# Hedgehog attention and an S4 convolution in one launch: the kernel written anew with shared stages, one hand-placed SBUF buffer and two half-width passes

## The chip, the cores and the metric

The kernel runs on one core of one Trainium2 chip. The metric is the device time of one execution in microseconds; six runs of the kernel before have a median of 710.55 us (710.0 to 714.23).

## The reference

Two independent parts write the two halves of one output of 2048 rows by 896 columns (bf16).

Part A (columns 0 to 447) is linear attention with 16 heads of 28: `q, k, v = x @ wqkv`; per head `pq = q @ w_phi[h]`, `pk = k @ w_phi[h]`; the features are `[softmax(pq), softmax(-pq)]` and the same of pk; `kv = sum_s phi_k^T v`, `z = sum_s phi_k`; `o = (phi_q @ kv) / (phi_q @ z + 1e-6)`; the output is `o @ wo`.

Part B (columns 448 to 895) is a state-space convolution: for 448 channels and 256 states `K[d, l] = Re sum_n C[d,n] * dt*B[d,n] * exp(dt*A[d,n]*l)`, then `y = irfft(rfft(u) * rfft(K))` over the sequence with zero padding, plus `u * Dskip`. The positions l are rounded to bf16, so only 641 distinct values of l occur.

## The kernel before

`hedgehog_attention` (L86 to L425) runs first. Four transposing loads bring x in as xT (L165). Eight groups of projections make qT and kT with channels on partitions (L181), sixteen make v (L196). Keys: for each of 16 row tiles one product with the block-diagonal w_phi (L217), two exponentials (L226), a sum per head (L228), a reciprocal and a product (L233). Queries: products (L254), two exponentials over 2048 columns (L263), normalisers by a matmul with head indicators (L270), a reciprocal on 16 partitions (L279), a broadcast back by matmul (L288) and a product (L295). The state kv is formed in 512 small matmuls (L312), goes through DRAM to become block-diagonal (L321, L338 to L342), and the denominators take another 16-partition reciprocal (L366). Numerators (L382), scaling (L399) and the output projection (L409) end part A.

`ssm_conv` (L507 to L836) follows, with its own loads of parameters and of u (L537 to L551). It makes parameters (L562 to L586), powers of exp(dt*A) (L611 to L633), and the spectrum SU of u by matmuls with a table G (L655, L657). K's 641 values come from factors: 32 coarse powers U (`hi_tables`, L699, on VectorE) times 49 fine powers W (`table_args`, L666: TensorE multiplies the exponents, ScalarE applies Exp into E and Sin twice into W). This runs for four quarters of the columns (L723). In each, E and W are filled, W is multiplied by E (L727, "damping"), and 448 small matmuls per quarter (L738) form K into Ts. After the last quarter 28 small DMAs on SP's queue scatter Ts into Kt (L749, L751), matmuls with tables `ft` give K's spectrum SK (L773, L775), and VectorE multiplies spectra (L786 to L833) between two inverse transforms (`inverse`, L799; matmuls L811; output L814 to L820).

Order on each engine is set by a planner: instructions carry their place in the program as priority, and among those that its own model holds ready, the earliest in the program is queued next. At run time each engine takes its queue in order. Buffers are tiles of pools; a tile that reuses another's bytes waits for it.

Of the kernel before, what the change touches and what calls it, by code (L numbers as in the profile page):

```python
# [11 lines left out]
I32 = mybir.dt.int32  # L13
ACT = mybir.ActivationFunctionType
ALU = mybir.AluOpType
AX = mybir.AxisListType

S_LEN = 2048
# [16 lines left out]
def round_f32(nc, out_ap, in_ap):
    nc.vector.tensor_scalar(out_ap, in_ap, MAGIC_ROUND, -MAGIC_ROUND, op0=ALU.add, op1=ALU.add)


def floor_div_const(nc, pool, out_ap, in_ap, shape, P, tag):
    t = pool.tile(shape, F32, name="fdt", tag=tag)
    nc.vector.tensor_scalar(t, in_ap, 1.0 / float(P), 0.5 / float(P) - 0.5, op0=ALU.mult, op1=ALU.add)
    round_f32(nc, out_ap, t)


def _head_row_segments(h):
    r0, r1 = D_HEAD * h, D_HEAD * h + D_HEAD
    segs = []
    for ci, plo, phi, g0, g1 in CHUNKS:  # L50
        a, b = max(r0, g0), min(r1, g1)
        if a < b:
            segs.append((ci, plo + (a - g0), plo + (b - g0), a - r0, b - r0))
    return segs


@with_exitstack
def kernel(
    ctx: ExitStack,
    tc: tile.TileContext,  # L60
    A_x: bass.AP,
    A_wqkv: bass.AP,
    A_w_phi: bass.AP,
    A_wo: bass.AP,
    B_u: bass.AP,
    B_A_re: bass.AP,
    B_A_im: bass.AP,
    B_B_re: bass.AP,
    B_B_im: bass.AP,
    B_C_re: bass.AP,  # L70
    B_C_im: bass.AP,
    B_log_dt: bass.AP,
    B_Dskip: bass.AP,
    out: bass.AP,
    do_a: bool = True,
    do_b: bool = True,
):
    nc = tc.nc
    out2 = out[0]
    if do_a:  # L80
        hedgehog_attention(tc, A_x, A_wqkv, A_w_phi, A_wo, out2)
    if do_b:
        ssm_conv(tc, B_u, B_A_re, B_A_im, B_B_re, B_B_im, B_C_re, B_C_im, B_log_dt, B_Dskip, out2)


def hedgehog_attention(tc, A_x, A_wqkv, A_w_phi, A_wo, out2):  # L86
    nc = tc.nc
    x2 = A_x[0]
    const_pool = tc.alloc_tile_pool(name="a_const", bufs=1)
    wt_pool = tc.alloc_tile_pool(name="a_w", bufs=1)  # L90
    va_pool = tc.alloc_tile_pool(name="a_va", bufs=1)
    work_pool = tc.alloc_tile_pool(name="a_work", bufs=2)
    small_pool = tc.alloc_tile_pool(name="a_small", bufs=2)
    dram_pool = tc.alloc_tile_pool(name="a_dram", bufs=1, space=bass.MemoryType.DRAM)

    dma_engs = [nc.sync, nc.scalar]
    dcount = [0]

    def dma(out_ap, in_ap, eng=None):
        if eng is None:  # L100
            eng = dma_engs[dcount[0] % len(dma_engs)]
            dcount[0] += 1
        return eng.dma_start(out=out_ap, in_=in_ap)

    Wt = []
    for j in range(4):
        t = wt_pool.tile([128, 3 * D_MODEL], BF16, name=f"Wqkv{j}")
        ci, plo, phi, g0, g1 = CHUNKS[j]
        dma(t[plo:phi, :], A_wqkv[g0:g1, :])
        Wt.append(t)  # L110
    Wo = []
    for j in range(4):
        t = wt_pool.tile([128, D_MODEL], BF16, name=f"Wo{j}")
        ci, plo, phi, g0, g1 = CHUNKS[j]
        dma(t[plo:phi, :], A_wo[g0:g1, :])
        Wo.append(t)
    WBD = []
    for j in range(4):
        t = wt_pool.tile([128, D_MODEL], BF16, name=f"WBD{j}")
        nc.gpsimd.memset(t[:, :], 0.0)  # L120
        WBD.append(t)
    for h in range(N_HEAD):
        for ci, plo, phi, s0, s1 in _head_row_segments(h):
            dma(WBD[ci][plo:phi, D_HEAD * h:D_HEAD * h + D_HEAD], A_w_phi[h, s0:s1, :])
    INDT16 = const_pool.tile([N_HEAD, D_MODEL], BF16, name="INDT16")
    it_f = small_pool.tile([N_HEAD, D_MODEL], I32, name="it_f", tag="it_f")
    nc.gpsimd.iota(it_f[:, :], pattern=[[1, D_MODEL]], base=0, channel_multiplier=0)
    ff = small_pool.tile([N_HEAD, D_MODEL], F32, name="ff", tag="ff")
    nc.vector.tensor_copy(ff[:, :], it_f[:, :])
    hd16 = small_pool.tile([N_HEAD, D_MODEL], F32, name="hd16", tag="hd16")  # L130
    floor_div_const(nc, small_pool, hd16[:, :], ff[:, :], [N_HEAD, D_MODEL], D_HEAD, "fd16")
# [36 lines left out]
    qT = []
    kT = []
    with tc.tile_pool(name="ps_qkv", bufs=1, space=bass.MemoryType.PSUM) as ps_pool:  # L170
        for which in range(2):
            for fc in range(4):
                ci, plo, phi, g0, g1 = CHUNKS[fc]
                frows = phi - plo
                fcol0 = which * D_MODEL + g0
                pool = qk_pool if which == 0 else k_pool
                dst = pool.tile([128, S_LEN], BF16, name=("qT" if which == 0 else "kT") + str(fc))
                ps = ps_pool.tile([128, S_LEN], F32, name="ps_qk", tag="big")
                for sc in range(4):
# [12 lines left out]
                (qT if which == 0 else kT).append(dst)
# [18 lines left out]
    for sgn in (+1, -1):  # L211
        PHIK[sgn] = phi_pool.tile([128, 16, D_MODEL], BF16, name=f"PHIK{'p' if sgn>0 else 'n'}")
# [654 lines left out]
```

## Time and profile before

| what | value |
|---|---|
| median of six runs | 710.55 us |
| the profiled execution's own time | 710.85 us |
| its span, first to last instruction | 709.1 us |
| mean granted TensorE clock (1 is 2.4 GHz, 0.5 is 1.2 GHz) | 0.727 |
| busy: TensorE, VectorE, ScalarE, GpSimd | 375.4, 401.1, 257.7, 9.6 us |
| DMA traffic | 17.19 MB, mean 24 GB/s |

The span is read by stages: a time window gives each engine's busy time in it, and the engine nearest to the window's length, or the chain of waits where none is near, is its bound. The profiled execution took 1.75 us more than its span, outside the first and last instruction.

### The profile page before, as it was taken

The numbers are of one execution on the slowest core, as the hardware profiler recorded it, in microseconds if no ns is written. First come the engines' busy times: TensorE is split into PE (matmuls) and PEld (weight loads), VectorE is DVE, ScalarE is ACT, GpSimd is POOL, SyncE is SP. The second block draws the span as 40 slices with busy tenths as digits, with TensorE's granted clock in tenths as the row PEclk, the third lists the DMA queues.
The fourth block names the chain that finished last, engine by engine and source line by source line (L and its number), as shares of the span: only waits on it lengthen the run. The fifth ranks groups of instructions, "written<-read, shape, count | busy, mean of one in ns | idle before, by whom it ended". The sixth has DMA issues, their size and how long they took to land.

```text
span 709.1 us, 8560 instructions
## 1 busy us (share of the span) xinstructions
PE 375.4 (53%) x3530; PEld 178.0 (25%) x3536; DVE 401.1 (57%) x576; ACT 257.7 (36%) x415; POOL 9.6 (1%) x31
## 2 busy tenths in 40 slices
PE   0599766453458464992537903624534326097434
PEld 0122211110015211231212502613424315043211
DVE  2043399205695137336462199886986983058981
ACT  0012134430000001221829993993884961053000
POOL 2000000010000000000000000000000000000000
PEclk9999955555556665996666955956857857589867
DMA  5300000000000000017200000000000020230101
GB/s 137 73 1 0 0 1 0 0 0 0 0 1 4 6 1 0 1 66 225 77 14 0 1 0 1 3 0 2 2 0 2 2 103 3 30 108 1 52 0 52
DMA packets 26622, 17.19 MB, mean 24 GB/s; under 512 B 15904, under 2 KB 25368, under 8 KB 26456
## 3 DMA queue, kind: packets, MB, share of 16 engines
q1 hardware_dynamic: 19098, 13.94, 7.2%
q10 hardware_dynamic: 7486, 2.72, 1.5%
q8 instruction: 27, 0.44, 0.3%
q14 instruction: 11, 0.09, 0.0%
HBM read 10.25 MB, written 3.72 MB: 20 GB/s over the span
## 4 chain that ended last, share of the span: by engine, by line
PE 34%; DVE 26%; ACT 18%; DMA 9%; issue 6%; SPq 5%; ACTq 1%; DVEq 0%
ACT W L679 11%; DVE W L727 7%; PE ps_k L738 6%; PE ps_qk L181 5%; PE num_ps L382 3%; PE ps_s L773 3%; PE ps_pq L254 3%; DMA xT<-in_A_x_dram 2%; DVE zk L228 2%; SPq L749 2%; SPq L551 2%; PE ps_u L655 2%; PE ps_o L811 2%; PE ps_a L673 2%; PE zps L270 2%
## 5 line engine op out<-in xcount | busy, mean ns | idle before, releaser
L738 PE MATMUL ps_k<-W,U 128*32 128x49 bf16 x1792 | 44.1, 268 | 46.8 <-DVE W L727 40.9
L673 PE MATMUL ps_a<-TH,PID 128*128 128x224 bf16 x128 | 20.3, 323 | 71.4 <-ACT W L679 70.2
L398 ACT CAST rbc_sb<-rbc_ps 128x512 bf16<-128x512 f32 (+1 forms) x16 | 9.2, 584 | 133.9 <-PE rbc_ps L391 133.5
L738 PEld LDWEIGHTS <-U 128*32 128x32 bf16 x1792 | 41.2, 138 | 50.1 <-issue 44.6
L181 PE MATMUL ps_qk<-xT,Wqkv 128*128 128x512 bf16 (+3 forms) x125 | 37.2, 405 | 29.2 <-DMA xT<-in_A_x_dram 26.0
L679 ACT ACTIVATE W<-ps_a,bias_hp 128x896 bf16<-128x896 f32 (+2 forms) x76 | 51.2, 822 | 0.4
L727 DVE TENSOR_TENSOR W<-W,E 128x10976 bf16<-128x10976 bf16 x8 | 46.6, 5871 | 8.1 <-ACT W L679 8.1
L673 PEld LDWEIGHTS <-PID 128*128 128x128 bf16 x256 | 29.4, 117 | 81.7 <-issue 76.5
L655 PE MATMUL ps_u<-ab,G 128*128 128x448 bf16 x128 | 33.4, 413 | 25.4 <-ACT SU L657 17.6
L679 ACT ACTIVATE E<-ps_a 128x896 bf16<-128x896 f32 (+2 forms) x76 | 46.0, 719 | 1.4 <-PE ps_a L673 1.3
L679 ACT ACTIVATE W<-ps_a 128x896 bf16<-128x896 f32 (+2 forms) x76 | 44.7, 819 | 0.0
L811 PE MATMUL ps_o<-SD,G 128*128 128x448 bf16 x128 | 27.8, 382 | 25.9 <-DVE SD L801 25.9
L710 DVE TENSOR_TENSOR t<-U,PW 128x896 bf16<-128x896 bf16 (+3 forms) x56 | 37.8, 675 | 2.0
L711 DVE TENSOR_TENSOR t<-U,PW 128x896 bf16<-128x896 bf16 (+3 forms) x56 | 37.5, 669 | 0.0
L773 PE MATMUL ps_s<-Kt,ft 128*128 128x448 bf16 x112 | 24.5, 381 | 18.1 <-DMA Kt<-Ts 18.0
L217 PE MATMUL ps_pk<-WBD,kT 128*128 128x448 bf16 x64 | 25.2, 508 | 15.7 <-ACT ek L226 13.6
L786 DVE TENSOR_TENSOR t<-SU,SK 128x3584 bf16<-128x3584 bf16 x6 | 12.0, 2020 | 37.7 <-ACT SK L775 37.6
L254 PE MATMUL ps_pq<-qT,WBD 128*128 128x512 bf16 (+3 forms) x39 | 18.7, 609 | 15.0 <-ACT EQ_n L263 11.3
L226 ACT ACTIVATE ek<-ps_pk 128x448 bf16<-128x448 f32 x32 | 16.8, 543 | 25.8 <-DVE PHIKp L233 22.6
L775 ACT CAST SK<-ps_s 128x448 bf16<-128x448 f32 x32 | 15.5, 545 | 27.4 <-PE ps_s L773 27.4
L655 PEld LDWEIGHTS <-G 128*128 128x128 bf16 x128 | 14.0, 110 | 42.6 <-issue 35.3
L181 PEld LDWEIGHTS <-Wqkv 128*128 128x128 bf16 (+3 forms) x128 | 11.0, 101 | 54.7 <-issue 46.1
(141 smaller groups left out, 627.2 us busy)
## 6 DMA issues: line engine op xcount, KB each, us to landing
ft<-dft_f SPq DMA_DIRECT2D x4, 896.0 KB
G<-dft_g SPq DMA_DIRECT2D x1, 1024.0 KB
out_dram<-osb ACTq DMA_DIRECT2D x8, 112.0 KB
out_dram<-osb SPq DMA_DIRECT2D x8, 112.0 KB
UD<-in_B_u_dram SPq DMA_DIRECT2D x4, 224.0 KB
UD<-in_B_u_dram SPq DMA_DIRECT2D x8, 112.0 KB
out_dram<-ob SPq DMA_DIRECT2D x4, 224.0 KB
out_dram<-ob SPq DMA_DIRECT2D x8, 112.0 KB
```

The costliest lines, as they stand in the source:

```text
L181: nc.tensor.matmul(ps[plo:phi, sc * 512:(sc + 1) * 512], lhsT=Wt[dci][dplo:dphi, fcol0:fcol0 + frows], rhs=xT[dci][dplo:dphi, sc * 512:(sc ...
L217: nc.tensor.matmul(ps[:, 0:D_MODEL], lhsT=kT[dci][dplo:dphi, tt * 128:(tt + 1) * 128], rhs=WBD[dci][dplo:dphi, 0:D_MODEL], start=(dj == 0) ...
L254: nc.tensor.matmul(ps[plo:phi, sc * 512:(sc + 1) * 512], lhsT=WBD[dci][dplo:dphi, g0:g0 + frows], rhs=qT[dci][dplo:dphi, sc * 512:(sc + 1) ...
L655: nc.tensor.matmul(ps[:, 0:D_MODEL], lhsT=G[:, cp, jt, 128 * mt:128 * mt + 128], rhs=ab[:, b, cp ^ st, jt, :], start=(jt == 0), stop=(jt = ...
L673: nc.tensor.matmul(o, lhsT=PID[:, 4 * grp + e, :], rhs=src[:, part, q0:q0 + 2 * COLS], start=(part == 0), stop=(part == 1))
L679: act(out_ap, in_ap, fn, scale=float(sgn * s), **kw)
L710: TT(out=t1[:, 0:n], in0=src, in1=bc(0), op=ALU.mult)
L711: TT(out=t2[:, 0:n], in0=src, in1=bc(1), op=ALU.mult)
L727: TT(out=W[:, ri, :, :], in0=W[:, ri, :, :], in1=E[:, :, :], op=ALU.mult)
L738: nc.tensor.matmul(ps[32 * g:32 * g + 32, qq * N_LO:(qq + 1) * N_LO], lhsT=U[:, :, ri, x], rhs=W[:, ri, :, (c % 2) * COLS + x], start=(i = ...
L773: nc.tensor.matmul(ps[:, 0:D_MODEL], lhsT=ft[:, fi, 128 * mt:128 * mt + 128], rhs=Kt[:, kt, :], start=(n == 0), stop=(n == len(terms) - 1))
L811: nc.tensor.matmul(ps[:, 0:D_MODEL], lhsT=G[:, cp, mt, 128 * jt:128 * jt + 128], rhs=S[:, r, cp, mt, :], start=(cp == 0 and mt == 0), stop ...
```

## The change

Nearly every line of the kernel's body is replaced; the two functions become one. What differs, in program order (names as in the new code):

1. **Buffers.** All of SBUF is one tile; `Bytes` cuts views of it at byte offsets chosen by hand, so that views of different stages lie on the same bytes. PSUM pools of a later stage wait per tile.
2. **Queues.** ACT's queue loads the state-space parameters, SP's the transposed x, GpSimd's the tables and weights; wo and G wait on GpSimd's queue for the last transpose.
3. **Weights folded.** `fold_weights` multiplies w_phi into the q and k columns of wqkv; q and k themselves are no longer formed.
4. **Keys.** One loop over 16 row tiles makes pk, v, both exponentials, one sum over both signs, and v divided by the sums; kv and z accumulate in one PSUM tile over the tiles, and a head mask makes them block-diagonal. No DRAM, no 512 small matmuls.
5. **SU** is stored to DRAM (`SUd`) in two halves of channels and read back late.
6. **Queries** keep plain exponentials; normalisers and denominators are formed with rows on partitions (128 matmuls of 8 columns), and one scale per row, sign and head (SC) goes into the numerators.
7. **Quarters.** `hi_tables` works once per quarter on 224 columns in place of twice on 112. Damping is cut into ten pieces issued as groups of W are finished. U has two buffers. The argument tiles still have two PSUM buffers.
8. **Halves.** After quarters 0-1 and 2-3 a half of the channels is scattered (24 + 4 DMAs, the 24 alternating between SP's and GpSimd's queue), and `kernel_spectrum` and `conv_half` work on 224 columns each; the first spectrum stands in the program behind the third quarter.
9. **Convolution.** u*Dskip is added by an identity matmul into PSUM and ScalarE evicts; u is read a second time on GpSimd's queue, 12 loads, into bytes of W.

The diff, cut to what the prediction speaks of:

```diff
+    sb = Bytes(sb_pool.tile([128, 211136 // 2], BF16, name="sbuf"))
+    ps_mm = ctx.enter_context(tc.tile_pool(name="ps_mm", bufs=2, space=bass.MemoryType.PSUM))
+    ps_a = tc.alloc_tile_pool(name="ps_a", bufs=1, space=bass.MemoryType.PSUM, reuse_waits="tile")
...
+    for k in (32, 64, 128):
+        for key, src in (("a", AT), ("t", TH)):
+            for half in range(2):
...
+                if key == "a":
+                    act(amp[:, hc], p[:, 0:D_MODEL], ACT.Exp, scale=float(k))
+                else:
+                    act(cs[:, 0, hc], p[:, 0:D_MODEL], ACT.Sin, scale=float(k), bias=bias_hp[:, :])
+                    act(cs[:, 1, hc], p[:, 0:D_MODEL], ACT.Sin, scale=float(-k))
...
+    acc = ps_a.tile([112, 2, 512], F32, name="acc", tag="acc")
+    for tt in range(16):
+        ts = slice(128 * tt, 128 * tt + 128)
+        pk = ps_a.tile([128, 512], F32, name="pk", tag="pk", bufs=2)
+        pv = ps_a.tile([128, 512], F32, name="pv", tag="pv", bufs=2)
+        for dj in range(4):
+            mm(pk[:, 0:D_MODEL], lhsT=xT[dj][:, ts], rhs=WpK[:, dj, :], start=(dj == 0), stop=(dj == 3))
+            mm(pv[:, 0:D_MODEL], lhsT=xT[dj][:, ts], rhs=wv[:, dj, :], start=(dj == 0), stop=(dj == 3))
+        EK = sb("EK", [128, 2, D_MODEL], BF16, oEK, bufs=2)
+        for s in range(2):
+            act(EK[:, s, :], pk[:, 0:D_MODEL], ACT.Exp, scale=1.0 - 2.0 * s)
+        zk = sb("zk", [128, 2, 16], F32, 10496, bufs=1)
+        nc.vector.tensor_reduce(zk[:, :, :], EK[:, :, :].rearrange("p s (h f) -> p s h f", f=D_HEAD), axis=AX.X,
+                                op=ALU.add)
+        nc.vector.reciprocal(rk[:, :, :], zk[:, :, :])
...
+        TT(out=VR[:, :, :, 0:D_HEAD],
+           in0=pv[:, 0:D_MODEL].rearrange("p (h d) -> p h d", d=D_HEAD).unsqueeze(1).to_broadcast(
+               [128, 2, 16, D_HEAD]),
+           in1=rk[:, :, :].unsqueeze(3).to_broadcast([128, 2, 16, D_HEAD]), op=ALU.mult)
...
+    for tt in range(16):
+        pn = ps_a.tile([128, 2, 512], F32, name="pn", tag="acc")
+        for s in range(2):
+            for c in range(4):
+                mm(pn[:, s, 112 * c:112 * c + 112], lhsT=EQ[:, s, c, ts], rhs=KVN[:, s, c, :, :],
+                   start=True, stop=True)
+        on = sb("on", [128, 2, D_MODEL], BF16, 0, bufs=2)
+        TT(out=on[:, :, :].rearrange("p s (h d) -> p s h d", d=D_HEAD),
+           in0=pn[:, :, 0:D_MODEL].rearrange("p s (h d) -> p s h d", d=D_HEAD),
+           in1=SC[:, tt].unsqueeze(3).to_broadcast([128, 2, 16, D_HEAD]), op=ALU.mult)
+        po = mmt([112, 4, 128])
+        for c in range(4):
+            for s in range(2):
+                mm(po[:, c, :], lhsT=on[:, s, 112 * c:112 * c + 112], rhs=ident, start=(s == 0), stop=(s == 1))
...
+    def damp_after(grp):
+        if grp == 0:
+            damp([slice(0, 4), slice(16, 20), slice(24, 32), slice(36, 40), slice(44, 49)])
+        elif grp == 1:
+            damp([slice(4, 8), slice(20, 24), slice(32, 36), slice(40, 44)])
+        elif grp == 3:
+            damp([slice(8, 16)])
...
+    for qt in range(4):
+        h = qt // 2
...
+        table_args(AT, qt, [E], [(ACT.Exp, None)], lambda g: None)
+        U = hi_tables(qt)
+        table_args(TH, qt, [W[:, 0], W[:, 1]], [(ACT.Sin, bias_hp[:, :]), (ACT.Sin, None)], damp_after)
+        build_k(qt, U, Ts)
+        if qt == 2:
+            kernel_spectrum(0, SKs[0])
+            nc.sync.dma_start(out=SUs[0][:, :, :, :, :, :], in_=SUd[:, 0])
...
+        if qt % 2 == 1:
+            scatter_k(h, Ts)
+            SK = sb(f"SK{h}", [128, 2, 2, 2, 4, HW], BF16, (oSK0, oW)[h])
+            if h == 1:
+                kernel_spectrum(h, SK)
...
+            UD = sb("UD", [128, 2, 2, 4, D_MODEL], BF16, oW + 14336)
...
+        for t in range(4):
+            nc.gpsimd.dma_start(out=UD[:, b, 1, t, :], in_=pair_rows(u2, 1024 * b, t, 0))
...
+    for h in range(2):
+        conv_half(h, SUs[h], SKs[h], UD, G2, OB)
```

## Rows read from the trace of the kernel before

**Rows 1.** The page: busy time by engine, and the chain's shares by engine.
```profile
PE 375.4 (53%) x3530; PEld 178.0 (25%) x3536; DVE 401.1 (57%) x576; ACT 257.7 (36%) x415; POOL 9.6 (1%) x31
...
PE 34%; DVE 26%; ACT 18%; DMA 9%; issue 6%; SPq 5%; ACTq 1%; DVEq 0%
```

**Rows 2.** Windows: length, busy us (count) PE, PEld, DVE, ACT, POOL; clock, DMA.
```profile
82.00:326.00 244.00, 148.85 (x870) 48.11 (x872) 122.23 (x183) 46.70 (x65) 3.36 (x8) 0.66 0.03 9
326.00:408.00 82.00, 45.34 (x232) 23.96 (x233) 37.78 (x68) 54.30 (x84) 1.21 (x4) 0.73 0.21 59
408.00:602.00 194.00, 75.97 (x2000) 65.39 (x1999) 157.23 (x229) 133.85 (x230) 0.00 (x0) 0.68 0.03 11
602.00:644.00 42.00, 23.95 (x118) 11.12 (x110) 12.13 (x8) 14.41 (x30) 0.00 (x0) 0.76 0.24 58
644.00:709.10 65.10, 28.50 (x132) 13.51 (x130) 48.66 (x45) 1.53 (x4) 0.00 (x0) 0.76 0.10 28
```

**Rows 3.** Timeline of one quarter: start, us, engine, line, operation, count, [idle before].
```profile
457.72 6.55 ACT L679 ACTIVATE W<-ps_a,bias_hp 128x896 bf16<-128x896 f32 x13
...
469.20 3.92 ACT L679 ACTIVATE W<-ps_a,bias_hp 128x896 bf16<-128x896 f32 x4
...
479.06 0.91 ACT L679 ACTIVATE W<-ps_a 128x896 bf16<-128x896 f32 x1
...
479.20 11.66 DVE L727 TENSOR_TENSOR W<-W,E 128x10976 bf16<-128x10976 bf16 x2 [2.69 <-ACT W L679]
...
490.91 3.70 PE L738 MATMUL ps_k<-W,U 128*32 128x49 bf16 x155 [5.40 <-DVE W L727]
...
503.30 1.71 PE L673 MATMUL ps_a<-AT,PID 128*128 128x224 bf16 x16
...
507.60 4.86 ACT L679 ACTIVATE W<-ps_a,bias_hp 128x896 bf16<-128x896 f32 x8
```

**Rows 4.** Groups by form: count | busy us, mean ns of one | idle before.
```profile
L711 DVE TENSOR_TENSOR t<-U,PW 128x1792 bf16<-128x1792 bf16 x16 | 17.4, 1085 | 0.0
...
L622 DVE TENSOR_TENSOR PW<-amp,cs 128x896 bf16<-128x896 f32 x4 | 4.1, 1086 | 0.0
...
L228 DVE TENSOR_REDUCE zk<-ek 128x16 f32<-128x448 bf16 x32 | 18.3, 614 | 9.7 <-ACT ek L226 9.7
...
L203 DVE CAST v_aug<-ps_v 128x448 bf16<-128x448 f32 x16 | 9.6, 622 | 14.8 <-PE ps_v L196 14.8
...
L232 DVE RECIPROCAL rzk<-zk 128x16 f32<-128x16 f32 x32 | 5.9, 226 | 0.0
...
L226 ACT ACTIVATE ek<-ps_pk 128x448 bf16<-128x448 f32 x32 | 16.8, 543 | 25.8 <-DVE PHIKp L233 22.6 <-PE ps_pk L217 3.1
...
L657 ACT CAST SU<-ps_u 128x448 bf16<-128x448 f32 x32 | 17.5, 588 | 4.7 <-PE ps_u L655 4.7
...
L679 ACT ACT_TABLE_LOAD x8 | 10.3, 1283 | 34.5 <-DVE W L727 33.7 <-PE ps_a L673 0.8
```

**Rows 5.** Timeline: TensorE runs whose length gives the pace of one matmul.
```profile
339.77 0.36 PE L584 MATMUL ps_t<-PID,natcr 112*128 112x112 bf16 x4
...
371.36 3.14 PE L655 MATMUL ps_u<-ab,G 128*128 128x448 bf16 x8 [12.36 <-ACT SU L657]
...
419.44 1.65 PE L673 MATMUL ps_a<-TH,PID 128*128 128x224 bf16 x8 [12.20 <-ACT W L679]
...
684.78 13.66 PE L811 MATMUL ps_o<-SD,G 128*128 128x448 bf16 x64 [21.56 <-DVE SD L801]
```

**Rows 6.** Timeline: what SP's queue needs to issue loads, scatter and outputs.
```profile
331.24 9.83 SPq L551 DMA_DIRECT2D UD<-in_B_u_dram  x4
...
602.66 4.14 SPq L749 DMA_DIRECT2D Kt<-Ts  x6
...
694.59 5.90 SPq L820 DMA_DIRECT2D out_dram<-ob  x4
```

**Rows 7.** Chain of waits, 0 to 30 us: start, us, what.
```profile
14.98 4.34 DMA xT<-in_A_x_dram
```

More of the change, by code (lines that the diff above doesn't have):

```diff
@@ L47, in _head_row_segments @@
[L47 to L83, printed above, removed]
@@ L504, in pair_rows, with __init__, __call__, kernel @@
                    ap=[[128 * rs, 2], [-2 * rs, 64], [1, D_MODEL]])
-def ssm_conv(tc, B_u, B_A_re, B_A_im, B_B_re, B_B_im, B_C_re, B_C_im, B_log_dt, B_Dskip, out2):
+class Bytes:
+    def __init__(self, tile_):
+        self.tile = tile_
+        self.turn = {}
+    def __call__(self, name, shape, dtype, off, bufs=1):
+        size = int(np.prod(shape[1:])) * (4 if dtype == F32 else 2)
+        turn = self.turn.get(name, 0)
+        self.turn[name] = turn + 1
+        a = (off + size * (turn % bufs)) // 2
+        v = self.tile[0:shape[0], a:a + size // 2]
+        if dtype == F32:
+            v = v.bitcast(F32)
+        names = "abcdefg"[:len(shape) - 1]
+        if len(names) > 1:
+            v = v.rearrange(f"p ({' '.join(names)}) -> p {' '.join(names)}",
+                            **{n: s for n, s in zip(names[1:], shape[2:])})
+        return v
+@with_exitstack
+def kernel(
+    ctx: ExitStack,
+    tc: tile.TileContext,
+    A_x: bass.AP,
+    A_wqkv: bass.AP,
+    A_w_phi: bass.AP,
+    A_wo: bass.AP,
+    B_u: bass.AP,
+    B_A_re: bass.AP,
+    B_A_im: bass.AP,
+    B_B_re: bass.AP,
+    B_B_im: bass.AP,
+    B_C_re: bass.AP,
+    B_C_im: bass.AP,
+    B_log_dt: bass.AP,
+    B_Dskip: bass.AP,
+    out: bass.AP,
+):
     nc = tc.nc
+    out2 = out[0]
+    x2 = A_x[0]
     u2 = B_u[0]
-    G_np, F_np, P_np = _dft_tables()
+    TT = nc.vector.tensor_tensor
+    act = nc.scalar.activation
+    mm = nc.tensor.matmul
+    G_np, F_np, P_np, M_np = _dft_tables()
     G_d = nc.inline_tensor(G_np, name="dft_g").ap()
@@ L607, in ssm_conv @@
-    sq = {}
-    amps = {}
-    for k in (32, 64, 128):
-        amps[k] = pw.tile([128, NCOL], F32, name=f"amp{k}")
-        act(split(amps[k][:, :]), args["a"], ACT.Exp, scale=float(k))
-    for k in (32, 64, 128):
-        s = pw.tile([128, 2, NCOL], F32, name=f"cs{k}")
-        act(split(s[:, 0, :]), args["t"], ACT.Sin, scale=float(k), bias=bias_hp[:, :])
-        act(split(s[:, 1, :]), args["t"], ACT.Sin, scale=float(-k))
-        sq[k] = s
-    for k in (32, 64, 128):
-        dst = PW[k]
-        if k == 128:
-            dst = pw.tile([128, 2, NCOL], F32, name="q128")
-        for ri in range(2):
-            TT(out=dst[:, ri, :], in0=amps[k][:, :], in1=sq[k][:, ri, :], op=ALU.mult)
@@ new lines @@
+    for sc in range(4):
+        for c in range(4):
+            p = ps_a.tile([112, 512], F32, name="pq", tag="pk", bufs=2)
+            for dj in range(4):
+                mm(p[:, :], lhsT=WpQ[:, dj, 112 * c:112 * c + 112], rhs=xT[dj][:, 512 * sc:512 * sc + 512],
+                   start=(dj == 0), stop=(dj == 3))
+            for s in range(2):
+                act(EQ[:, s, c, 512 * sc:512 * sc + 512], p[:, :], ACT.Exp, scale=1.0 - 2.0 * s)
+    for hb in range(2):
+        p = mmt([128, 8, 2, 4, 8])
+        for t8 in range(8):
+            ts = slice(128 * (8 * hb + t8), 128 * (8 * hb + t8) + 128)
+            for s in range(2):
+                for c in range(4):
+                    mm(p[:, t8, s, c, :], lhsT=EQ[:, s, c, ts], rhs=KVZ[:, s, c, :, :], start=True, stop=True)
+        ndv = p[:, :, :, :, :].rearrange("p t s c (h z) -> p t s (c h) z", z=2)
+        nc.vector.reciprocal(rz[:, :, :, :], ndv[:, :, :, :, 1])
+        TT(out=dz[:, :, :, :], in0=ndv[:, :, :, :, 0], in1=rz[:, :, :, :], op=ALU.mult)
+        nc.vector.scalar_tensor_tensor(out=den[:, 0], in0=dz[:, :, 0, :], scalar=1e-6, in1=dz[:, :, 1, :],
+                                       op0=ALU.add, op1=ALU.add)
+        nc.vector.reciprocal(den[:, 1], den[:, 0])
+        TT(out=SC[:, 8 * hb:8 * hb + 8], in0=rz[:, :, :, :],
+           in1=den[:, 1].unsqueeze(2).to_broadcast([128, 8, 2, 16]), op=ALU.mult)
@@ L695, in table_args @@
-                    emit(dst[:, 48, :], ps[:, 0, 0:2 * COLS], 128)
+                        emit(dst[:, st, :], one[i], 32)
+                    emit(dst[:, 45, :], one[0], 64)
+                    emit(dst[:, 48, :], one[0], 128)
                 elif grp == 1:
-                    emit(pair(40, 4), full, 8)
-    def hi_tables(c):
-        U = tp.tile([128, N_HI, 2, COLS], BF16, name="U", tag="U")
-        nc.vector.tensor_copy(U[:, 0, :, :], CBc[:, c, :, :])
+                    emit(four(40), full, 8)
@@ new lines, in table_args, with damp @@
+            done(grp)
+    def damp(lo_aps):
+        for sl in lo_aps:
+            w = W[:, :, sl, :].rearrange("p r l x -> p r (l x)")
+            e = E[:, sl, :].rearrange("p l x -> p (l x)").unsqueeze(1)
+            n = w.shape[2]
+            TT(out=w, in0=w, in1=e.to_broadcast([128, 2, n]), op=ALU.mult)
+    def damp_after(grp):
[5 more added lines that the diff above has]
+            damp([slice(8, 16)])
@@ L721, in hi_tables, with build_k @@
         return U
-    for qt in range(4):
-        table_args(AT, qt, [E], [(ACT.Exp, 1, None)])
-        table_args(TH, qt, [W[:, 0], W[:, 1]], [(ACT.Sin, 1, bias_hp[:, :]), (ACT.Sin, 1, None)])
-        for ri in range(2):
-            TT(out=W[:, ri, :, :], in0=W[:, ri, :, :], in1=E[:, :, :], op=ALU.mult)
-        for c in (2 * qt, 2 * qt + 1):
-            U = hi_tables(c)
+    def build_k(qt, U, Ts):
+        for c in range(2):
             for hq in range(2):
-                ps = ps_kb.tile([128, 512], F32, name="ps_k", tag="kb")
+                p = ps_t.tile([128, 512], F32, name="kb", tag="kb", bufs=2)
                 for qq in range(7):
@@ new lines, in scatter_k, with half, kernel_spectrum @@
+                r += n
+        for g in range(4):
+            nc.sync.dma_start(out=Kt[0:1, 5, 112 * g + 56 * h:112 * g + 56 * h + 56],
+                              in_=Ts[32 * g + 31:32 * g + 32, 48, :])
+    def half(t, h):
+        return t.rearrange("p (g h x) -> p h g x", g=4, h=2)[:, h]
+    def kernel_spectrum(h, SK):
+        for st_cp in range(4):
+            cp, st = st_cp // 2, st_cp % 2
+            for mp in range(2):
+                fts = []
+                for mt in (2 * mp, 2 * mp + 1):
+                    ft = sb("ft", [128, 7, 128], BF16, ft_at())
+                    nc.sync.dma_start(out=ft[:, :, :], in_=F_d[4 * st_cp + mt])
+                    fts.append(ft)
@@ new lines @@
+    for b in range(2):
+        for a in range(2):
+            nc.gpsimd.dma_start(out=UD[64 * a:64 * a + 64, b, 0, :, :], in_=rep_rows(u2, 1024 * b, a, 0))
+        for t in range(4):
+            nc.gpsimd.dma_start(out=UD[:, b, 1, t, :], in_=pair_rows(u2, 1024 * b, t, 0))
+        TT(out=UD[:, b], in0=UD[:, b], in1=DSK[:, :].unsqueeze(1).unsqueeze(1).to_broadcast([128, 2, 4, D_MODEL]),
+           op=ALU.mult)
+    ps_t.release()
+    ps_y = tc.alloc_tile_pool(name="ps_y", bufs=1, space=bass.MemoryType.PSUM, reuse_waits="tile")
```

852 lines of the change are left out of this document (298 added, 554 removed).

## The prediction

> **What bounds the kernel now.** I read the page's busy line first: 375.4 us on TensorE, 401.1 on VectorE and 257.7 on ScalarE in 709.1 us, so 1.46 engines are at work on average and none is the bound of the whole; the chain says the same, shared out 34%, 26% and 18% [rows 1]. So the windows come next. From 82 to 326 us (part A behind the projections) VectorE is busy for half the time, TensorE for 61% at a clock of 0.66, ScalarE for a fifth: they wait on each other in turn. From 326 to 408, the preparation of part B, no engine passes two thirds. From 408 to 602, the four quarters, VectorE is at 81% and ScalarE at 69%. From 602 to 709 there is a scatter, a spectrum and a convolution one behind the other [rows 2]. The timeline of one quarter shows its chain: W's activations from 457.72 to 479.97, damping to 490.86, K's matmuls to 503.3, then 4.3 us to the next W at 507.60; the period is 49.6 to 49.9 us [rows 3].
>
> **The change as a sum.** The sum goes along the span of the new kernel, stage by stage. Each stage has a floor and a ceiling from rows. VectorE costs 1.085 us for 1792 bf16 elements and 1.086 for 896 in fp32 [rows 4], so about 2.0 for 3584 bf16.
>
> Start. The four transposes still follow each other at 4.34 us [rows 7], 17 us together, now at the front of SP's queue. Alone they would end at 19; the other first loads, now on two further queues, share the DMA engines with them. I take 25 (19 to 33). The folding of weights and most of the parameter arithmetic lie beside it.
>
> Keys. Per row tile VectorE has a sum over 896 (twice 0.614, 1.15 where two follow closely), a reciprocal of 32 (0.33 by the 0.226 for 16) and a product of 896 from PSUM (1.09, by 0.622 for 448 and about 1.04 ns for each further element): 2.6 us, times 16 is 41.6 [rows 4]. The powers share VectorE here: three products of 1792 fp32 (2.0 each) and six operations of 896 (1.09), 12.6; weights and masks 3. Together 57. ScalarE has 33 us of powers and table loads and 16 times 1.3, less than that. TensorE has 8 matmuls of 448 and 8 of 116 a tile: 1.95 us at 2.4 GHz (187 and 50 ns), 3.7 at 1.2 GHz (373 and 93), from runs of 64 in 13.66, of 4 in 0.36 and of 8 in 3.14 us [rows 5]. So 57 (42 if the powers hide, 69 at the low clock): at 82.
>
> SU and queries. These have no order between them once the keys are done, so I take the longest engine: ScalarE, 32 evictions at 0.588 and 32 exponentials of 512 at 0.60 (0.543 for 448) [rows 4] are 38, with hops 41. TensorE needs 128 x 0.187 + 64 x 0.213 = 38 at the high clock, and 75 at the low one. u arrives in time: its 6 loads a batch take 11.3 us, 4 of them 9.83 [rows 6], after the powers free their bytes at some 62. At 123.
>
> Scales and output of part A. 4 us remain of the denominators. Each of 16 tiles has one numerator buffer: matmuls 0.43, VectorE 1.09, hops 0.3, so no less than 1.85 us a tile, 30 in all; with TensorE at 1.2 GHz a tile needs 16 x 0.093 + 4 x 0.373 = 3.0, 48 and some fill, 55. I take 44, near the middle, since no row tells which of the two levels these short matmuls get. The 26.5 us of U and E's table (11.5 us) of the first quarter fit beside it. At 171 W starts.
>
> Quarters. W's activations stay: 22.2 us [rows 3]. Damping now trails the groups. The first group's sines end 11.4 us after W starts (469.20 less 457.72), its five pieces (three of 1792, one of 3584, one of 2240 elements) take 6.6; the next four pieces 4.3, ready at 18.2; the last 2.0, ready at 22.2. So damping ends at 24.6 if nothing of U stands before it, and up to 2 us later if one operation does; 24.9 to 26.6 with hops. It was 33.1. The gain is 8.3 and, with half an obstacle, 8. K's matmuls (12.5) and the 4.3 us behind them stay, so a period is 41.3 (40.3 to 49.6, the old one, if nothing is gained). VectorE has 39.3 a quarter now (157.2 over four [rows 2]), a little less with longer operations; it fits, at 94%. Three periods are 124, the last quarter without its tail 37.6. The first half's spectrum, 112 matmuls of 224 and 16 evictions, falls between the third quarter and the fourth: 8.7 us if only ScalarE counts, 23 if TensorE at 1.2 GHz does (0.206 a matmul, 8 in 1.65 [rows 5]). I take 12. At 344.6 K is done.
>
> Tail. Scatter: 28 issues at 0.69 (6 in 4.14 [rows 6]); 16 of them remain on SP, 10.9, and 1.7 to land: 12.6. No row shows a transfer issued by GpSimd; its 12 may take 0.69 each as on SP or, like u's row loads, 2.46 each, so 8 to 30. I take SP's, since these are the same transfers. Spectrum: 112 x 0.117 at the high clock and one eviction, 13.7 (112 x 0.206 = 23 at the low). The first half's convolution hides in those 26 us on VectorE (27 us, part of it before). Then the second: six products at 2.0, two sums, and ten results of 1792 in all, 27, less one product that starts early, 25; the last inverse, 72 x 0.117, 8.4; eviction and stores 10 (5.90 to issue four [rows 6], as now); hops 3. Sum 72.7 (62 to 92). Before, this stretch took 107 us.
>
> In all 25 + 57 + 41 + 48 + 174 + 72.7 = 417 us of span, and 1.75 us outside it, as now: 419 for the profiled execution, which stands 0.3 above the median of 710.55. The prediction is 419 us.
>
> By the Trainium skill, "SBUF — State Buffer", section "SBUF: two separate sides", a DMA issued from GpSimd has its descriptors written by GpSimd, which is shut out while VectorE runs an operation in a two-port mode. The trace of before cannot show it, since only SP and ACT issue. That rule speaks against item 2 and against u's second load, and its time is the second rival's.
>
> **The rivals.**
> 1. TensorE stays at 1.2 GHz through part A. For: from 82 to 326 the granted clock is 0.66 on average, in small groups of matmuls between waits [rows 2]. Against: the run of 64 in 13.66 us at the end is at 2.4 GHz [rows 5], and the new groups are longer. Price: keys +12, queries +34, output +11, so 476.
> 2. GpSimd's queue is late. Scatter's half and then u's 12 loads stand on it while VectorE runs the 27 us of the first convolution. Identity matmuls need u, and TensorE's queue is in order. Price: the transfers wait for that stretch, some 25 us, so 444. The rule above would give this.
> 3. The pieces of damping don't trail: one piece reaches over both halves of W, and if the next group's sines wait for it, or if VectorE, at 94%, always has U in front, the quarter stays at 49.6. Price 4 x 8 = 33 less the last's share, so 444 to 452.
> 4. Better: GpSimd's and ScalarE's spare time takes more. With an argument buffer free early, the first W runs beside part A's output (ScalarE has 18 of 44 us there), -15, and the spectrum costs its 8.7, -3; the transposes -6: 395.
> 5. Slower than before: views of one tile are taken for their whole stretch of bytes, and the planner makes engines wait that share none. Then work runs one engine at a time. VectorE's list is about 332 us (16 parameters, 13 powers, 42 keys, 25 rest of A, 106 U, 49 damping, 54 convolution, 27 other), ScalarE's 310 (145 tables, 10 loads of them, 30 powers, 125 other), TensorE's about 350: 990. It decides when fewer than 990/710 = 1.39 engines work on average; before has 1.46. Against it, weakly: before, VectorE writes strided parts of U while TensorE reads another U of the same pool, and neither waits [rows 3, 4].
>
> **How the numbers follow.** The forecast, 395 to 440, has 0.42; rival 1 0.16, rival 2 0.14, rival 3 0.10, rival 4 (375 to 395) 0.13, rival 5 0.05. The range leaves out rival 5, the lower end of rival 4 and the upper end of 1: 378 to 482, about 8 in 10. A measurement of this kernel tells some 0.3% from none. Faster 0.94 (all but rival 5 and a margin), same 0.01, slower 0.05.
>
> **What would show it.** Keys: 16 tiles in 55 to 60 us with VectorE nearly full. Queries: ScalarE full for 40 us. Quarters: W to W in 40 to 43 us, with the last damping piece no more than 4 us behind the last sine. Between K's last matmul and the first spectrum matmul of the second half 13 us. Wrong would be: a TensorE clock near 0.6 through the first 170 us; identity matmuls waiting on u; a period near 50; ScalarE reloading tables tens of times where Exp of the keys meets Sin of the powers (1.283 each [rows 4], the first stage only).

## The result, and the profile after

The kernel after takes 455.5 us (454.8 to 456.2, eight runs) against 710.9 for the kernel before: ratio 0.641, 95% interval 0.639 to 0.642. The forecast was 419 (378 to 482): the direction and the range held, the point was 36 us too low. Its profiled execution has a span of 457.0 us. That is some 3 us more than the median implies, and 2.1 to 3.8 of them lie ahead of the first W: it starts at 208.6 here, and at 204.8 to 206.5 in the four experiments below that change nothing before it.

Page of the kernel after, busy line and chain, to be read against [rows 1]:

```profile
PE 280.7 (61%) x3592; PEld 203.6 (45%) x3592; DVE 303.1 (66%) x317; ACT 282.1 (62%) x514; POOL 35.0 (8%) x63
...
PE 33%; ACT 25%; DVE 19%; SPq 9%; DMA 7%; issue 5%; DVEq 0%; ACTq 0%
```

TensorE and VectorE are busy for about a quarter less time, ScalarE for a tenth more, and (280.7 + 303.1 + 282.1) / 457.0 = 1.9 engines work on average where 1.46 did. TensorE's share is not work alone: its mean granted clock rose from 0.727 to 0.813. Windows of the kernel after, by the stages of the forecast (columns as in [rows 2]): keys to queries, output of part A, E of the first quarter, the four quarters, the second scatter, the rest of the tail:

```profile
26.60:154.00 127.40, 99.54 (x674) 55.64 (x675) 97.62 (x119) 87.52 (x159) 2.96 (x8) 0.89 0.19 61
154.00:195.50 41.50, 34.46 (x346) 21.87 (x347) 27.59 (x36) 17.34 (x31) 0.00 (x0) 0.92 0.26 83
195.50:208.60 13.10, 6.30 (x42) 4.99 (x40) 13.00 (x11) 12.10 (x21) 0.47 (x1) 0.74 0.03 9
208.60:378.10 169.50, 89.47 (x2113) 77.01 (x2113) 124.47 (x121) 141.76 (x246) 7.56 (x13) 0.73 0.16 48
378.10:397.60 19.50, 8.02 (x62) 6.19 (x61) 5.32 (x7) 0.98 (x2) 15.86 (x24) 0.67 0.67 117
397.60:457.00 59.40, 38.82 (x341) 35.37 (x341) 29.07 (x22) 16.80 (x47) 0.00 (x0) 0.79 0.27 69
```

Length of each against the forecast: 127.4 against 98, 41.5 against 48, 13.1 against none (hidden), 169.5 against 173.6, 19.5 against 12.6, 59.4 against 60.1; the start took 26.6 against 25. These differences add up to 39.7 us, the whole miss of the profiled execution. Three of them make it, the first, the third and the fifth: 49.4 us together, of which the shorter stages give 11.3 back.

A quarter of the kernel after in the timeline, against [rows 3]:

```profile
208.61 6.55 ACT L447 ACTIVATE sbuf<-arg,sbuf 128x896 bf16<-128x896 f32 x13
...
230.69 0.92 ACT L447 ACTIVATE sbuf<-arg 128x896 bf16<-128x896 f32 x1
...
249.31 6.55 ACT L447 ACTIVATE sbuf<-arg,sbuf 128x896 bf16<-128x896 f32 x13
...
216.00 2.09 DVE L473 TENSOR_TENSOR sbuf<-sbuf 128x1792 bf16<-128x1792 bf16 x2 [3.15 <-ACT sbuf L447]
...
231.64 2.02 DVE L473 TENSOR_TENSOR sbuf<-sbuf 128x3584 bf16<-128x3584 bf16 x1 [2.69 <-ACT sbuf L447]
```

The first damping piece starts 7.4 us after W starts, the last ends at 233.66, 25.1 us after W starts and 2 after the last sine; the period is 40.7 us (forecast 41.3; it was 49.6).

### The profile page after: what moved, and what is told of

It is laid out like the page before. It is cut to its first block, busy times and chain, and to the rows that moved or that the text cites. A ratio compares the mean times of both kernels' runs of the same rounds, so it can differ in the third digit from the quotient of the medians.

```text
span 457.0 us, 8549 instructions
## 1 busy us (share of the span) xinstructions
PE 280.7 (61%) x3592; PEld 203.6 (45%) x3592; DVE 303.1 (66%) x317; ACT 282.1 (62%) x514; POOL 35.0 (8%) x63
## 4 chain that ended last, share of the span: by engine, by line
PE 33%; ACT 25%; DVE 19%; SPq 9%; DMA 7%; issue 5%; DVEq 0%; ACTq 0%
ACT sbuf L447 13%; PE kb L517 9%; DVE sbuf L473 6%; PE mmt L368 5%; SPq L207 5%; PE mmt L555 5%; DMA sbuf<-in_B_u_dram 4%; PE pq L378 3%; DVE sbuf L581 3%; PE mmt L416 3%; PE mmt L411 2%; PE yo L602 2%; SPq L531 2%; DVE sbuf L495 2%; DVE sbuf L494 2%
## 5 line engine op out<-in xcount | busy, mean ns | idle before, releaser
L447 ACT ACTIVATE sbuf<-arg 128x896 bf16<-128x896 f32 (+2 forms) x152 | 86.5, 759 | 3.7 <-PE arg L440 2.0
L440 PE MATMUL arg<-sbuf 128*128 128x224 bf16 x256 | 39.8, 319 | 69.4 <-ACT sbuf L447 69.4
L440 PEld LDWEIGHTS <-sbuf 128*128 128x128 bf16 x256 | 30.0, 119 | 77.3 <-issue 72.7
L473 DVE TENSOR_TENSOR sbuf<-sbuf 128x1792 bf16<-128x1792 bf16 (+2 forms) x40 | 49.9, 1297 | 8.4 <-ACT sbuf L447 8.3
L447 ACT ACTIVATE sbuf<-arg,sbuf 128x896 bf16<-128x896 f32 (+2 forms) x76 | 51.2, 822 | 1.0 <-PE arg L440 0.9
L517 PE MATMUL kb<-sbuf 128*32 128x49 bf16 x1792 | 43.4, 269 | 8.9 <-DVE sbuf L473 5.6
L517 PEld LDWEIGHTS <-sbuf 128*32 128x32 bf16 x1792 | 41.3, 140 | 11.6 <-issue 10.3
L495 DVE TENSOR_TENSOR sbuf<-sbuf 128x1792 bf16<-128x1792 bf16 (+3 forms) x28 | 32.9, 1187 | 7.9 <-PE mmt L368 5.0
L602 PE MATMUL yo<-sbuf 128*128 128x224 bf16 x256 | 32.5, 279 | 6.5 <-DVE sbuf L592 6.5
L555 PEld LDWEIGHTS <-sbuf 128*128 128x128 bf16 x224 | 23.7, 109 | 27.1 <-issue 18.0
L557 ACT CAST sbuf<-mmt 128x448 bf16<-128x448 f32 x32 | 16.0, 556 | 29.8 <-PE mmt L555 29.8
L494 DVE TENSOR_TENSOR sbuf<-sbuf 128x1792 bf16<-128x1792 bf16 (+3 forms) x28 | 33.2, 1187 | 0.8
L602 PEld LDWEIGHTS <-sbuf 128*128 128x128 bf16 x256 | 26.4, 105 | 8.3 <-issue 6.7
L370 ACT CAST sbuf<-mmt 128x448 bf16<-128x448 f32 x32 | 17.0, 533 | 16.5 <-PE mmt L368 16.3
L368 PEld LDWEIGHTS <-sbuf 128*128 128x128 bf16 x128 | 12.7, 100 | 23.5 <-issue 13.3
```

The lines of the kernel that those rows point to most:

```text
L368: mm(p[:, 0:D_MODEL], lhsT=G1[:, cp, jt, 128 * mt:128 * mt + 128], rhs=ab[:, cp ^ st, jt, :], start=(jt == 0), stop=(jt == 3))
L440: mm(p[:, e // 2, (e % 2) * QC:(e % 2 + 1) * QC], lhsT=PID[:, 4 * grp + e, :], rhs=src[:, part, cols], start=(part == 0), stop=(part == 1))
L447: act(out_ap, in_ap, fn, scale=float(s), **kw)
L473: TT(out=w, in0=w, in1=e.to_broadcast([128, 2, n]), op=ALU.mult)
L494: TT(out=t2[:, 0:n], in0=src, in1=bc(1), op=ALU.mult)
L495: TT(out=dst, in0=src, in1=bc(0), op=ALU.mult)
```

## The experiments

**What the parts cost alone.** One kernel leaves out all of part B, the other all of part A.

> Leaves out all of part B (its half of the output is not written): what part A costs alone. Theory (the change is mostly less work and shorter chains within each part): about 140 us (125 to 165), since the start is 26.6, key tiles at VectorE's 2.6 us 42, queries 19, output 41 and some ends; before, part A ended at 326. Rival (it is mostly the two parts filling each other's waits): 200 us or more.

> Leaves out all of part A (its half of the output is not written): what part B costs alone. Theory: about 345 us (320 to 370), since the powers end near 60, SU near 100, and the 170 us of quarters and 79 of tail stay; with part A alone that makes a sum under 520, so at least 190 of the 255 us gained come from the parts themselves. Rival (overlap): the two alone sum to 600 or more.

Measured: 134.4 and 382.5 us, one run each; the second lies above its range. The windows of part A alone are keys (from the second tile's sum on) and queries, of part B alone SU and the first E:

```profile
35.80:77.60 41.80, 35.93 (x266) 19.33 (x266) 38.02 (x49) 22.03 (x52) 0.00 (x0) 1.00 0.00 1
77.60:91.00 13.40, 13.36 (x154) 8.85 (x152) 5.19 (x10) 11.99 (x25) 0.00 (x0) 1.00 0.01 2
```

```profile
60.00:129.00 69.00, 33.96 (x160) 17.29 (x161) 25.38 (x23) 37.35 (x57) 0.28 (x1) 0.74 0.21 74
```

The sixteen key tiles alone run from 33.0 to 76.9, which is 43.9 us with 2.4 us of weight casts among them; the forecast had 41.6 for them, and VectorE is at 91% in the first window. In its own window part B alone needs 69 us, with no engine at 55%, where some 40 were expected; VectorE waits there for u, 25.7 us in two waits. The two sum to 516.9: of the 255 us gained, some 194 come from the parts themselves and 61 from one filling the other's gaps. The split is rough, since each run pays a start of its own, and part A alone ran at a granted clock of 0.99, beside part B at 0.89 to 0.92. Within the 194, no run takes the folded weights, the merged key loop or the scales per row out one at a time, so what each of them gave is not shown; for the damping a run below shows it.

**u's first loads.** In the kernel after they lie on bytes of the powers, in one buffer, so the second batch also waits for the first products, which end at 94.81 (timeline: SP issues, then VectorE):

```profile
65.33 1.40 SPq L357 DMA_DIRECT2D sbuf<-in_B_u_dram  x2
78.28 5.29 SPq L359 DMA_DIRECT2D sbuf<-in_B_u_dram  x4
94.84 1.35 SPq L357 DMA_DIRECT2D sbuf<-in_B_u_dram  x2
96.25 6.50 SPq L359 DMA_DIRECT2D sbuf<-in_B_u_dram  x4
...
90.73 1.09 DVE L360 TENSOR_TENSOR sbuf<-sbuf 128x1792 bf16<-128x1792 bf16 x1 [3.46 <-DMA sbuf<-in_B_u_dram]
...
93.73 1.08 DVE L361 TENSOR_TENSOR sbuf<-sbuf 128x1792 bf16<-128x1792 bf16 x1
...
109.95 1.09 DVE L360 TENSOR_TENSOR sbuf<-sbuf 128x1792 bf16<-128x1792 bf16 x1 [6.68 <-DMA sbuf<-in_B_u_dram]
```

First try:

```diff
-        ua = sb("ua", [128, 2, 4, D_MODEL], BF16, ud0, bufs=1)
+        ua = sb("ua", [128, 2, 4, D_MODEL], BF16, oU1, bufs=2)
```

> u's first loads get two buffers in the bytes of EQ, which are free until the queries, in place of one buffer in bytes of the powers. Theory (the loads hold the stage up): in the kernel after, VectorE waits 3.5 and 6.7 us at the sums of u for these loads, TensorE and the rest of the key tiles stand behind; both waits go and the queries end some 10 us earlier: 445.5 us (440 to 450). Rival (the engines' own work fills the stage: TensorE is busy for 99.6 of the 127.4 us from 26.6 to 154.0): what is waited for now is waited for elsewhere, 452 us or more.

Measured: 456.2 us, no change. The loads came early, but the planner then put a product of u near the head of VectorE's queue, ahead of its load's arrival:

```profile
55.05 1.09 DVE L361 TENSOR_TENSOR sbuf<-sbuf 128x1792 bf16<-128x1792 bf16 x1 [18.75 <-DMA sbuf<-in_B_u_dram]
```

So the run says little on the theory: it traded two waits (10.1 us) for a longer one. Second try, with the products pinned behind the powers by their bytes:

```diff
+        ua = sb("ua", [128, 2, 4, D_MODEL], BF16, oU1, bufs=2)
-        ab = sb("ab", [128, 2, 4, D_MODEL], BF16, ud0 + 7168, bufs=2)
+        ab = sb("ab", [128, 2, 4, D_MODEL], BF16, ud0 + 3584, bufs=2)
```

> As e_u_early, but the sums and differences of u lie wholly in bytes of the powers, so that none of them can be queued on VectorE ahead of the powers; in e_u_early one stood there and held VectorE for 18.8 us until 55.1, which cost what the early loads gave. Theory (the loads held the stage up by 10 us): no wait of VectorE for u, 445.5 us (440 to 450). Rival (TensorE and ScalarE fill the stage anyway): 453 us or more.

Measured: 439.9 us (ratio 0.6205, 0.617 to 0.624), 14 us less than after by the ratios and just better than the theory's range; VectorE waits for u no more, and the first W starts at 191.3. The same window, keys to queries:

```profile
26.60:138.40 111.80, 93.97 (x665) 53.80 (x663) 96.04 (x118) 87.73 (x159) 1.14 (x4) 0.94 0.20 65
```

111.8 us in place of 127.4 with the same work: the theory holds. What is left above 98 is another thing: three engines at 84%, 86% and 78% of one window.

**E of the first quarter.** In the kernel after its exponentials (196.0 to 207.3) stand on ScalarE's queue behind the last copy of part A. Their place in the program alone does not explain it: U stands behind E there, and its operations on VectorE start at 95.0. What E lacks is PSUM: the first of the two argument buffers lies on the two banks of the numerators `pn`, which all 16 output tiles use, and E's first argument matmul starts 0.5 us after VectorE has read the last of them (timeline: U's first, then these):

```profile
94.99 0.15 DVE L487 COPY sbuf<-sbuf 128x224 bf16<-128x224 bf16 x1
...
192.06 1.08 DVE L405 TENSOR_TENSOR sbuf<-pn,sbuf 128x896 bf16<-128x896 f32 x1
...
193.69 0.83 PE L440 MATMUL arg<-sbuf 128*128 128x224 bf16 x7
...
195.98 9.47 ACT L447 ACTIVATE sbuf<-arg 128x896 bf16<-128x896 f32 x18
```

In the run below the arguments use single PSUM banks, those of `pv`, free since the keys, and stand in the program among part A's output tiles:

```diff
+    def early(src, grp, dsts, funcs):
+        for hf in range(2):
+            p = ps_a.tile([128, 512], F32, name="pv", tag="pv", bufs=2)
...
     for tt in range(16):
+        if tt in (0, 2, 4, 6):
+            early(AT, {0: 0, 2: 1, 4: 2, 6: 3}[tt], [E], [(ACT.Exp, None)])
         ts = slice(128 * tt, 128 * tt + 128)
```

> The first quarter's E is formed in single PSUM banks (those of pv) and stands in the program among the first 7 tiles of part A's output; the main loop leaves it out for that quarter. Theory (the first W starts late because E's 11.3 us of exponentials, 196.0 to 207.3, stand on ScalarE's queue behind all of part A's copies, while ScalarE was busy for 17.3 of 41.5 us before): W starts 8 to 13 us earlier, 444.5 us (442 to 448). Rival (the exponentials delay the copies between them, and the output of part A ends later by as much): 452 us or more.

Measured: 442.3 us (ratio 0.6223, 0.620 to 0.625), 13 less. These argument matmuls run from 135.1 on, before part A's output begins, and the first W follows the last copy at once (timeline, ScalarE):

```profile
192.99 0.53 ACT L454 CAST sbuf<-mmt 128x448 bf16<-128x448 f32 x1 [1.02 <-PE mmt L452]
193.54 1.28 ACT L482 ACT_TABLE_LOAD   x1
194.83 5.55 ACT L482 ACTIVATE sbuf<-arg,sbuf 128x896 bf16<-128x896 f32 x10
```

The run changes banks and place together; whether new banks in the old place would have done was not run.

**Damping in one go.** All ten pieces behind the last group:

```diff
-        if grp == 0:
-            damp([slice(0, 4), slice(16, 20), slice(24, 32), slice(36, 40), slice(44, 49)])
-        elif grp == 1:
-            damp([slice(4, 8), slice(20, 24), slice(32, 36), slice(40, 44)])
-        elif grp == 3:
-            damp([slice(8, 16)])
+        if grp == 3:
+            damp([slice(0, 4), slice(16, 20), slice(24, 32), slice(36, 40), slice(44, 49),
+                  slice(4, 8), slice(20, 24), slice(32, 36), slice(40, 44), slice(8, 16)])
```

> All ten pieces of the damping stand behind the last group of sines, as the kernel before had it; nothing else changes. Theory (the forecast's step: trailing pieces save 8 us a quarter): periods near 49, 4 x 8 = 32 us more, 487 us (480 to 497). Rival (VectorE is nearly full in a quarter, and what it no longer does during the sines it does for U instead, so that the order of its work is worth little): 464 us or less.

Measured: 477.9 us (ratio 0.672, 0.670 to 0.674), 22 more: between the two expectations. The first two periods are 47.8 and 48.1 us in place of 40.7 and 41.1, and the last quarter 45.9 in place of 37.9, as forecast; its chain shows why:

```profile
372.99 1.02 ACT sbuf L447
374.03 12.22 DVE sbuf L473 x10
386.30 3.82 PE kb L514 x149
```

But the third period is 51.2 against 49.8. The first half's spectrum stands in it: in the kernel after 70 of its 112 matmuls run behind K's (327.5 to 337.2) and hold the next W back, here all but 14 run while TensorE waits for the damping anyway, so there the trailing pieces are worth 1.4 us. The step saves 7 to 8 us in three quarters of four.

**The second scatter.** The chain of the kernel after, with K complete at 378.2:

```profile
378.66 0.85 SPq L531
...
389.30 0.74 SPq L535
390.08 7.36 DMA sbuf<-sbuf
397.58 4.90 PE mmt L555 x27
```

SP's 16 issues end at 390.8, 12 us after the first (forecast 10.9); the last transfer lands 6.6 us later (forecast 1.7), 7.4 after its issue began. Four runs on why. The first leaves out u's second load and u*Dskip:

> Leaves out the second load of u (12 transfers, 1.8 MB) and with it u*Dskip: zeros are written in its place. Theory (the second scatter lands 6.6 us after its last issue, where 1.7 were forecast, because u's transfers and the tables share the DMA engines with it): the scatter takes 13 to 14 in place of 19.5 us, and the time falls to 449.5 us (447 to 452). Rival 1 (SP's 16 issues set the scatter's end): 454 us or more. Rival 2 (GpSimd's queue is late with its half of the scatter, whatever else it has): 454 us or more, with the last wait on a transfer of GpSimd's.

Measured: 445.6 us (ratio 0.627, 0.624 to 0.629), 10 less. K is complete at 373.8 and the scatter's last transfer lands 1.8 us after its issue began:

```profile
384.98 1.77 DMA sbuf<-sbuf
...
389.10 1.13 PE mmt L555 x10
```

That is 13.0 us for the scatter, the theory's number. The trace's packets agree: this transfer of 0.1 KB is 14 packets of 8 bytes, which pass from 386.35 to 386.46 here; in the kernel after the last such packets straggle until 396.37. The tables were not taken out, so their share is not shown. The next two keep u:

```diff
-                    eng = (nc.sync, nc.gpsimd)[i % 2]
+                    eng = (nc.sync, nc.gpsimd)[i % 2] if h == 0 else (nc.gpsimd, nc.scalar, nc.sync)[i % 3 if i < 18 else i % 2]
```

> The second scatter's 24 transfers go out on three queues (9 on GpSimd's, 9 on ScalarE's, 6 on SP's, and the 4 of one row on SP's as before) in place of two. Theory (SP's issues last until 390.8, and u's second load starts at 385.9, so the last transfers share the DMA engines with it; issued by about 386, they land before it): the scatter takes 12 to 14 in place of 19.5 us, 449.5 us (446 to 452). Rival (a transfer may only be issued when the one eight issues earlier on these queues has landed, so more queues bring no more at a time): 454 us or more.

Measured: 450.8 us (ratio 0.6365, 0.633 to 0.640): a time in the theory's range, though the interval touches after's, but not by its mechanism. The scatter takes 17.2 us (374.7 to 391.8), not 12 to 14. Issues end 10.4 us after K in place of 12.6, and the one wait among ScalarE's for an earlier transfer holds them up for 0.6 us, so the rival's limit on issues is not what binds; u's loads start sooner as well, and the last transfer on ScalarE's queue, of 10.5 KB, takes longer still (chain):

```profile
382.96 8.68 DMA sbuf<-sbuf
```

Then, on the same three queues, u was held behind the scatter:

```diff
+    nc.gpsimd.tensor_copy(UD[:, :, :, :, 0], Kt[:, 5, 432:448].rearrange("p (b r t) -> p b r t", b=2, r=2))
     for b in range(2):
         for a in range(2):
             nc.gpsimd.dma_start(out=UD[64 * a:64 * a + 64, b, 0, :, :], in_=rep_rows(u2, 1024 * b, a, 0))
```

> e_three_q, and u's second load is held on GpSimd's queue behind a copy of 16 elements that reads the last row of the scatter, so that none of it shares the DMA engines with the scatter. Theory (sharing is what makes the scatter late: without u's load it took 13.0 us, on three queues with it 17.2): 11 to 14 us from K's end to the spectrum, 448.5 us (446 to 452). Rival (u, which now starts only when the scatter has landed, is late for its two products on VectorE and for the identity matmuls, and costs as much there): 453 us or more.

Measured: 453.8 us (ratio 0.639, 0.636 to 0.641), the rival's number. The scatter is short now (374.1 to 384.4), but u is late for its product and for the identity matmuls, and both queues stand:

```profile
401.09 2.03 DVE L665 TENSOR_TENSOR sbuf<-sbuf 128x3584 bf16<-128x3584 bf16 x1 [7.62 <-DMA sbuf<-in_B_u_dram]
403.17 0.34 PE L604 MATMUL yo<-sbuf 128*128 128x224 bf16 x1 [5.26 <-DVE sbuf L665]
```

**Together.** best1 is e_u_early2 with e_tab_early, and the first two groups of the first quarter's sines in single banks too:

> e_u_early2 and e_tab_early together, and the first two groups of the first quarter's sines too, in single banks among the tiles 8 to 15 of part A's output. Theory (these are separate waits, so their gains add: 15.7 and 13.2 us, and some 8 for the sines): 418 us (413 to 427). Rival (ScalarE and VectorE are full beside part A's output by then, and the sines' part and some of the exponentials' go back): 429 us or more.

Measured: 424.3 us (ratio 0.598, 0.595 to 0.601). If the two gains add, 14 and 13, the sines bring some 3 in place of 8 (no run has the two without the sines). ScalarE is then at 91% beside part A's output, which ends nearly 16 us later than in e_u_early2:

```profile
140.00:180.00 40.00, 26.72 (x269) 18.75 (x266) 23.64 (x29) 36.47 (x84) 0.00 (x0) 0.87 0.21 66
```

> best1 with e_hold's scatter on three queues and u held behind it. Theory (it adds e_hold's gain): best1 less 4 to 8 us, about 412 us (406 to 420). Rival (u's late arrival takes it back): best1 or more.

Measured: 426.0 us (ratio 0.600, 0.597 to 0.603), no better than best1: again the rival. Then u was loaded ahead of the scatter, and the scatter put on three queues:

```diff
             nc.gpsimd.dma_start(out=G2[:, :, :, :], in_=G_d)
+            UD = sb("UD", [128, 2, 2, 4, D_MODEL], BF16, 28672)
+            for b in range(2):
...
-            SU = sb(f"SU{h}", [128, 2, 2, 2, 4, HW], BF16, (oSU0, 28672)[h])
+            SU = sb(f"SU{h}", [128, 2, 2, 2, 4, HW], BF16, (oSU0, oW + 14336)[h])
+            UDo = sb("UDo", [128, 2, 2, 4, D_MODEL], BF16, oU1 + 14336)
-        TT(out=UD[:, b], in0=UD[:, b], in1=DSK[:, :].unsqueeze(1).unsqueeze(1).to_broadcast([128, 2, 4, D_MODEL]),
+        TT(out=UDo[:, b], in0=UD[:, b], in1=DSK[:, :].unsqueeze(1).unsqueeze(1).to_broadcast([128, 2, 4, D_MODEL]),
```

> best1, with u's second load moved out of the scatter's time: it goes into bytes of the powers, which the last quarter's U has done with some 45 us before K is complete, SU's second half takes its old place, its two products go to other bytes so that VectorE cannot be held at them before K is done, and the second scatter has three queues as in e_three_q. Theory (holding u back gained 8 us at the scatter and lost them at the identity matmuls, so u is needed early and out of the way; without u the tail was 10 us shorter): scatter 9 to 10 us, no wait for u, 412 us (408 to 416). Rival (the tail is then set by the tables' loads or by VectorE, and the gain is under 4 us): 420 us or more.

Measured: 419.2 us, ratio 0.5886 (0.586 to 0.591): the fastest, 6 to 7 us under best1 by the ratios and 36 under after, between the two expectations. From K's last copy to the end it takes 69.5 us, as without u (69.5; after 78.8, e_hold 77.8, best1 76.5). Behind the scatter, now 10.6 us, the load of SU's second half takes the place that u had (waits, from 343 us on); of the three things changed against best1 none was run alone:

```profile
DVE sbuf L624 <- DMA sbuf<-SUd: 10.7, 1, 10.7
```

## Why the prediction was right, and where it was short

- **Direction and range**: less time in each part and more of it side by side, as argued. The range held although three steps failed, since other stages came out shorter and hid 11.3 us of it. Rival 5 (views of one tile make engines wait) is out: 1.9 engines work on average, and it needed fewer than 1.39. Rival 4 (better, 395) did not come; one of its three parts did, the spectrum's price.
- **Start** 25: 26.6 in the profile. (The terms of the sum add up to 417.7, printed as 417.)
- **Keys** 57, **SU and queries** 41: together 127.4, the step that failed most. The key tiles were sized right (43.9 alone, 2.4 of it casts). Wrong was "u arrives in time": the forecast had the powers free the bytes at some 62, where the second part of the loads could go out at 78.3, and did not count that with one buffer the second batch waits for the first's products, nor that VectorE's in-order queue stands behind them. That is 14 us (e_u_early2). The other 14 is argued and no run tests it: the way of summing, the longest engine of each of two stages, 57 + 41. In one merged stage the three engines carry 88 to 96 us, 94 of it on TensorE, for which 69 stood in the working; the fullest two reached 84 and 86% of the window, not 100.
- **Scales and output** 48: 41.5. Rival 1 (TensorE low through part A) is out: the granted clock is 0.89 and 0.92 there, and 0.67 to 0.79 only behind it.
- **E of the first quarter beside the output**: wrong, 13 us, e_tab_early shows it. ScalarE did have the room. But the arguments that E is made from could not be written before the last numerators were read (193.1), as their buffer lies on those banks. The forecast put E's table beside the output without asking where its arguments would lie; only rival 4 named the argument buffer, and for W.
- **Quarters**: period 41.3 against 40.7 and 41.1, last 37.6 against 37.9, the spectrum's 12 against 8.9. Rival 3 (pieces don't trail) is out. The 8 us a quarter is right in three quarters; e_damp_whole shows that the spectrum's quarter had no use for it.
- **Tail** 72.7: 78.9. The scatter's issues were nearly right (12 us against 10.9), the landing was not (6.6 against 1.7). Rival 2 said "GpSimd's queue is late" and priced it at 25 us. Its queue was on time: 12 issues in 6.96 us beside SP's 12 in 8.94. What was late was the transfer, with u's loads on the same DMA engines: without them the scatter takes 13.0 us in place of 19.4, and the run 10 us less, with what waits for u on VectorE and TensorE (e_no_ud).

GpSimd's issues did not stall under VectorE: the first scatter's 12 took 0.62 to 0.68 us each while VectorE was busy for 9.0 of 9.2 us, all of it in bf16 `tensor_tensor` operations, the second's 0.59 to 0.66 with VectorE at half. By the Trainium skill, "SBUF — State Buffer", section "SBUF: two separate sides", the stall belongs to two-port operations, and `tensor_tensor` has no two-port mode. The trace agrees, and to read rival 2's time out of that rule was a mistake of the prediction, since VectorE's work beside the scatters and in the convolution is `tensor_tensor`.

## What to carry to other kernels

Before a stage is given its busiest engine's time, ask for each load when its bytes come free and what stands behind its first reader on that in-order queue. Room on an engine is of use only if the buffers that the work and its inputs need, PSUM banks too, are free by then; and a load made early is a gain only if its first reader is not moved up with it. A merged stage with three loaded engines is better summed over all its work than by each part's own bound; in the one measured here the fullest engine reached 86%.

## Of the hardware, unexpected

Small transfers suffer far more from company than their size says: the scatter's last transfer, of 0.1 KB, landed 1.8 us after its issue began in a scatter at 41 GB/s in all (e_no_ud), and 7.4 us after it with u's rows on the same DMA engines, at 117 GB/s (after). A third issuing queue ended the issues 2.2 us sooner and the scatter 2.2 us sooner, of 19.4.
